# Reordering the join of two spectral transforms, and two moves in the load queue, in an adaLN block on one core

## The chip, the cores and the metric

The kernel runs on one core of a Trainium2 chip. Times are device microseconds of one execution; the median of several is quoted. Two figures occur for one execution: the time (about 253 us) and the span of the profile (about 251 us, from the first to the last instruction). Positions such as "at 84 us" are on the profile's clock.

Engines are named as in the profile: PE is TensorE's matmuls, PEld its weight loads, DVE is VectorE, ACT is ScalarE, POOL is GpSimd, SP the engine that issues most DMAs, SPq its queue.

## The reference, cut to what matters

```python
mod = (_silu(c) @ w_mod).reshape(1, 6, 1, -1)      # sa, ca, ga, sb, cb, gb
h = _layernorm(x) * (1 + ca) + sa
x = x + ga * irfft2(rfft2(h) * (w_r + 1j * w_i))   # "A": spectral filter, 2048 x 640
h = _layernorm(x) * (1 + cb) + sb
x = x + gb * ((silu(h @ w_gate) * (h @ w_up)) @ w_down)   # "B": feed-forward, 640 -> 1728 -> 640
```

The kernel does the forward transform over the rows (to about 36 us), then 21 groups of frequencies pass a *join*: a first-stage product on TensorE, a multiplication by the weights on VectorE, a second stage back (to 63 us). The rest of the inverse transform makes 16 tiles of the new x (to 84 us). Then comes the feed-forward part in five chunks of rows, the first of which is computed in the plain way.

## The kernel before

The queue of loads that SP issues, in order, with cuts. A DMA transpose turns four blocks of the forward transform around. `wm_r` holds modulation weights.

```python
t2_dma(0); t2_dma(1); t2_dma(2)                                   # transposes, used from group 5 on
nc.sync.dma_start(wm_r[:, :, 1:3, :], wm_m[:, :, 1:3, :])         # 1600 KB
t2_dma(3)                                                         # used from group 17 on
nc.sync.dma_start(wm_r[:, :, 3, :], wm_m[:, :, 3, :])
# ... inverse table, w_down (2.2 MB), last gate/up slice ...
load_gu(0, 512)       # columns of w_gate, then of w_up
load_gu(512, 1024)
# ... in the loop over the 16 tiles of x:
if t == 5:
    ln2_tr(0)                # DMA transpose of the first chunk's normalised rows
    load_gu(1024, 1664)
if t in (8, 11):             # GpSimd's queue: sums of weights made by accumulating DMAs
    gu_dma(GS[0][:], B_w_gate, t // 11 * 2, 2, t == 8)
if t in (10, 13):
    ln2_mod(0, range(4) if t == 10 else range(4, 5))   # scaling of the transposed chunk: 4 on GpSimd, 1 on ScalarE
# ... after the loop: four more gu_dma (GS[2] and UG: gate, then up added onto it)
```

The join. `wsum` forms the sum of real and imaginary weights; the half `Wv` comes from a row-flipped copy of the weights that takes a detour through DRAM and lands late.

```python
ga_mod(320, 5, range(3))
t2_pe(0)
wsum(Wv, 48, 64, nc.vector)          # waits for the flipped weights
t2_pe(1)
ga_mod(320, 5, range(3, NC5))        # broadcast of the gate ga, 5 matmuls a half
PPs[0] = stage_a(0)                  # 4 matmuls, then prod(.., 0) with Wn and prod(.., 1) with Wv on VectorE
# ...
PPs[1] = stage_a(1)
ga_mod(0, 6, range(2))
for g in range(NG + 1):
    # ... weight sums for later groups, on GpSimd ...
    if g + 2 < NG:
        PPs[g + 2] = stage_a(g + 2)
    if g == 0:
        ga_mod(0, 6, range(2, NC5))
    # ...
    if g < NG:
        Y2s[g] = stage_b(g, PPs.pop(g))      # 8 matmuls, 1 ScalarE copy
    # ... stage_c, evacuation ...
```

The plain gate/up block of the first chunk takes its 13 slices of 128 columns in the order 0, 6, 1, 7, 2, 8, ...:

```python
for fc in range(NFC - 1):
    ff = fc if fc == 12 else fc // 2 + 6 * (fc % 2)
    half = gu_plain(ci, ATc, ff, (c3f, c22f)[fc % 2])
    half(0)      # 5 matmuls with gate columns
    half(1)      # 5 matmuls with up columns
```

## Time and profile before

| | before |
|---|---|
| time, three runs | 253.23 us median (251.34 to 253.86) |
| span of the profile | 250.8 us |
| TensorE busy, granted clock | 97%, 0.999 |

From the page of the kernel before: busy us of each engine with the share of the span, and the span in 40 slices of 6.3 us (a digit is tenths of busy time; PEclk is the granted clock in tenths).

```profile
PE 243.4 (97%) x2512; PEld 200.1 (80%) x2512; DVE 210.1 (84%) x524; ACT 163.1 (65%) x300; POOL 74.4 (30%) x122
PE   8899998999999999999999999999999999999994
PEclk9999999999999999999999999999999999999999
DMA  7999999999999999500005021002311000211001
```

TensorE is near full throughout, at full clock. The DMA engines are near full until about 100 us (the first 16 digits).

From VectorE's timeline before. Columns: start us, us, engine, line, operation, output<-input, count, and in brackets the idle time before it and what ended it.

```profile
39.27 0.43 DVE L407 TENSOR_TENSOR rW<-rW 128x512 bf16<-128x512 bf16 x1 [1.13 <-DMA rW<-wflip_r]
39.62 5.33 DVE L588 TENSOR_TENSOR rM<-psum,rW 128x384 bf16<-128x384 f32 x12
45.14 4.74 DVE L588 TENSOR_TENSOR rM<-psum,rW 128x384 bf16<-128x384 f32 x10 [0.20 <-PE psum L567]
```

The sum of the late weights (L407) starts when their DMA lands, after 1.13 us of idling; twelve products follow without a break.

From TensorE's timeline before:

```profile
40.68 0.49 PE L567 MATMUL psum<-Ktab,rM 128*128 128x192 bf16 x4 [0.99 <-DVE rM L588]
82.41 0.49 PE L972 MATMUL psum<-rW,Wp 128*128 128x256 bf16 x3
83.22 0.38 PE L972 MATMUL psum<-rW,Wp 128*128 128x256 bf16 x2 [0.32 <-POOL rW L784]
83.98 14.36 PE L984 MATMUL psum<-rW 128*128 128x256 bf16 x130
98.17 7.80 PE L877 MATMUL psum<-rA,rX 128*128 128x320 bf16 x56
```

There is a hole of 0.99 us in the join, and one of 0.32 us inside the last gate/up slice (L972), which waits for GpSimd's scaling. The plain gate/up block (L984) starts at 83.98 and runs its 130 matmuls without a hole: 14.19 us to the first down product.

From the chain of waits before (start us, us, what): the second norm's transpose takes 6.46 us from issue to landing, and GpSimd's scaling follows.

```profile
74.12 6.46 DMA rW<-rL
80.76 0.55 POOL rW L784
81.31 1.87 POOL rW L784 x3
84.15 14.19 PE psum L984 x130
```

From the list of DMA issues before (KB each, us from issue to landing): the fourth transpose, and the last up load (columns 1024 on).

```profile
rM<-rA SPq DMA_TRANSPOSE x1, 10.5
rW<-in_B_w_up_dram SPq DMA_DIRECT2D x1, 800.0 KB, 9.3
```

### The profile page before, as it was taken

How to read it: one execution, taken by the hardware profiler on the slowest of the kernel's cores; microseconds unless marked ns; L12 is line 12 of the kernel's file. 1: busy time of each engine (PE TensorE's matmuls, PEld its weight loads, DVE VectorE, ACT ScalarE, POOL GpSimd, SP SyncE). 2: the span in 40 equal slices, each digit the busy share in tenths (PEclk: the TensorE clock that was granted, in tenths of full speed). 3: DMA queues.
4: the chain of work that ended last, by engine and by line, in shares of the span. 5: the costliest groups of instructions: out<-in, count | busy, mean ns of one | idle time of the engine just before them, and what ended most of it. 6: DMA issues, size and time to landing. Idle time of an engine off the chain costs nothing.

```text
span 250.8 us, 6472 instructions
## 1 busy us (share of the span) xinstructions
PE 243.4 (97%) x2512; PEld 200.1 (80%) x2512; DVE 210.1 (84%) x524; ACT 163.1 (65%) x300; POOL 74.4 (30%) x122
## 2 busy tenths in 40 slices
PE   8899998999999999999999999999999999999994
PEld 3678877999889888788877778886768887779973
DVE  4698888998898997779997997879995888895895
ACT  3678756988788787678963577774257676235740
POOL 8477766677021805000001910001330000440000
PEclk9999999999999999999999999999999999999999
DMA  7999999999999999500005021002311000211001
GB/s 204 400 338 327 308 386 182 269 270 398 301 343 273 238 270 183 119 26 0 3 0 107 0 78 31 3 3 41 77 42 52 3 0 3 52 54 56 3 0 52
DMA packets 45760, 34.43 MB, mean 137 GB/s; under 512 B 21731, under 2 KB 42658, under 8 KB 45346
## 3 DMA queue, kind: packets, MB, share of 16 engines
q1 hardware_dynamic: 43936, 30.00, 42.4%
q0 software_dynamic: 1504, 3.95, 7.0%
q8 instruction: 19, 0.31, 0.5%
q10 hardware_dynamic: 290, 0.08, 0.1%
q14 instruction: 11, 0.09, 0.1%
HBM read 26.72 MB, written 4.72 MB: 125 GB/s over the span
## 4 chain that ended last, share of the span: by engine, by line
PE 68%; DMA 12%; SPq 9%; issue 4%; DVE 2%; POOL 2%; ACT 0%; DVEq 0%; POOLq 0%; ACTq 0%
PE psum L1014 32%; PE psum L897 19%; PE psum L984 9%; DMA rM<-rA 4%; DMA rW<-wflip_r 4%; PE psum L877 3%; DMA rW<-rL 3%; SPq L273 2%; SPq L277 2%; DMA rM<-in_w_mod_dram 2%; SPq L275 2%; PE psum L972 2%; SPq L279 2%; PE psum L595 1%; PE psum L567 1%
## 5 line engine op out<-in xcount | busy, mean ns | idle before, releaser
L1014 PEld LDWEIGHTS <-rW 128*128 128x128 bf16 (+1 forms) x528 | 46.9, 98 | 5.7 <-issue 0.2
L1014 PE MATMUL psum<-rW 128*128 128x256 bf16 (+1 forms) x240 | 27.1, 259 | 0.0
L911 POOL TENSOR_TENSOR rM<-rM,rL 128x320 f32<-128x320 f32 x6 | 5.9, 976 | 68.3 <-ACT rL L910 68.3
L897 PEld LDWEIGHTS <-rE 128*128 128x128 f16 (+1 forms) x196 | 19.1, 97 | 7.7
L1014 PE MATMUL psum<-rY,rW 128*128 128x256 bf16 (+1 forms) x96 | 24.0, 259 | 0.0
L984 PE MATMUL psum<-rW 128*128 128x256 bf16 (+1 forms) x170 | 23.1, 291 | 0.0
L897 PE MATMUL psum<-rE 128*128 128x320 f16 (+1 forms) x147 | 22.3, 299 | 0.0
L588 DVE TENSOR_TENSOR rM<-psum,rW 128x384 bf16<-128x384 f32 (+2 forms) x42 | 20.0, 541 | 1.8 <-PE psum L567 0.9
L984 PEld LDWEIGHTS <-rW 128*128 128x128 bf16 x170 | 16.6, 98 | 3.8
L1014 PEld LDWEIGHTS <-rE 128*128 128x128 f16 x192 | 17.4, 98 | 2.4
L897 PEld LDWEIGHTS <-rX 128*128 128x128 bf16 (+1 forms) x151 | 14.6, 97 | 5.4
L1050 DVE TENSOR_TENSOR rH<-psum,rW 128x512 bf16<-128x512 f32 x21 | 14.5, 690 | 4.9 <-PE psum L1014 3.1
L758 POOL TENSOR_TENSOR rstd<-rstd,mhalf 128x4 f32<-128x4 f32 (+2 forms) x4 | 4.7, 1187 | 46.7 <-DVE rstd L754 46.7
L1046 ACT COPY rH<-psum 128x512 f32<-128x512 f32 x21 | 12.3, 586 | 8.7 <-PE psum L1014 7.0
L1053 ACT COPY rX<-psum 128x512 f32<-128x512 f32 x21 | 12.3, 587 | 6.9 <-PE psum L1014 6.9
L1040 ACT COPY rW<-psum 128x512 f32<-128x512 f32 x21 | 12.3, 586 | 6.8 <-PE psum L1014 6.6
L1068 DVE TENSOR_TENSOR rX<-rH,rL 128x512 bf16<-128x512 bf16 x21 | 8.9, 424 | 9.1 <-ACT rL L1066 9.0
L382 DVE SCALAR_TENSOR_TENSOR rE<-rE,mv,psum 128x648 bf16<-128x648 f32 (+1 forms) x17 | 14.2, 844 | 2.6 <-PE psum L318 1.5
L1054 DVE TENSOR_TENSOR rX<-psum,rX 128x512 f32<-128x512 f32 x21 | 14.4, 685 | 1.7 <-ACT rX L1053 1.6
L897 PE MATMUL psum<-rA,rX 128*128 128x320 bf16 (+1 forms) x98 | 15.6, 299 | 0.0
L1014 PE MATMUL psum<-rH,rW 128*128 128x256 f16 (+1 forms) x96 | 15.1, 259 | 0.1
L1014 PE MATMUL psum<-rE,rY 128*128 128x256 f16 (+1 forms) x96 | 15.1, 259 | 0.0
(198 smaller groups left out, 675.3 us busy)
## 6 DMA issues: line engine op xcount, KB each, us to landing
out_dram<-rA SPq DMA_DIRECT2D x31, 80.0 KB, 1.6
rM<-in_w_mod_dram SPq DMA_DIRECT2D x3, 800.0 KB, 9.8
rX<-in_A_x_dram SPq DMA_DIRECT2D x3, 640.0 KB, 7.9
rA<-in_B_w_down_dram SPq DMA_DIRECT2D x2, 960.0 KB, 9.9
rM<-in_w_mod_dram SPq DMA_DIRECT2D x1, 1600.0 KB, 8.1
rY<-in_B_w_gate_dram POOLq DMA_DIRECT2D x2, 768.0 KB, 7.2
rW<-in_B_w_gate_dram SPq DMA_DIRECT2D x2, 640.0 KB, 8.0
rW<-in_B_w_up_dram SPq DMA_DIRECT2D x2, 640.0 KB, 8.2
```

What stands on the lines that cost most here:

```text
L382: nc.vector.scalar_tensor_tensor(Zv[:, h], Cv[:, h], mv[:, t, 0:1], zps[:, h], ALU.mult, ALU.subtract)
L588: nc.vector.tensor_tensor(PP[:, :, hl], xv[:, :, hl], in1, ALU.mult)
L877: nc.tensor.matmul(pop, lhsT=ATc[rows(k), k, tl * 128:(tl + 1) * 128], rhs=Wd_sb[rows(k), k, 320 * h:320 * h + 320], start=(k == 0), stop= ...
L897: nc.tensor.matmul(o, lhsT=lhsT, rhs=rhs, start=start, stop=stop, skip_group_check=True)
L984: nc.tensor.matmul(gu[u], lhsT=Wgu[:, u, c5, ff * 128:(ff + 1) * 128], rhs=h2T[:, :, c5, :], start=(c5 == 0), stop=(c5 == NC5 - 1))
L1014: nc.tensor.matmul(o[:, f], lhsT=w, rhs=b, start=(start and f == 0 and i == 0), stop=(stop and f == F - 1 and i == len(ops) - 1), skip_gro ...
L1040: nc.scalar.copy(c0, X)
L1046: nc.scalar.copy(c2, X)
L1050: nc.vector.tensor_tensor(c11, Z, c0, ALU.add)
L1053: nc.scalar.copy(c3, X)
L1054: nc.vector.tensor_tensor(c22, Y, c3, ALU.add)
L1068: nc.vector.tensor_tensor(ato, v4(c11), v4(g21), ALU.mult)
```

## The change

The intent is to close those holes: let the first product run before VectorE waits for the late weights, fill TensorE's hole with gate-broadcast matmuls, and bring two transposes forward in the queue by letting two weight loads stand behind them.

```diff
@@ SP's queue
         t2_dma(2)
+        t2_dma(3)
         nc.sync.dma_start(wm_r[:, :, 1:3, :], wm_m[:, :, 1:3, :])
-        t2_dma(3)
@@ stage_a (the modulation columns, which read wm_r[1:3], move to later groups)
-    for c5 in {NG - 6: (0, 1), NG - 5: (0, 1), NG - 4: (2, 3), NG - 3: (2,), NG - 2: (4,), NG - 1: (3, 4)}.get(g, ()):
+    for c5 in {NG - 4: (0, 1), NG - 3: (0, 1), NG - 2: (2, 3, 4), NG - 1: (2, 3, 4)}.get(g, ()):
...
             prod(g, PP, xps, 0)
+            if g == 0:
+                wsum(Wv, 48, 64, nc.vector)
             prod(g, PP, xps, 1)
@@ the join
         t2_pe(0)
-        wsum(Wv, 48, 64, nc.vector)
...
-        ga_mod(0, 6, range(2))
+        ga_mod(0, 6)
         for g in range(NG + 1):
...
+            if g == 0:
+                Y2s[0] = stage_b(0, PPs.pop(0))
             if g + 2 < NG:
                 PPs[g + 2] = stage_a(g + 2)
-            if g == 0:
-                ga_mod(0, 6, range(2, NC5))
...
-            if g < NG:
+            if 0 < g < NG:
                 Y2s[g] = stage_b(g, PPs.pop(g))
@@ gate/up loads
     load_gu(0, 512)
-    load_gu(512, 1024)
...
                 ln2_tr(0)
+                load_gu(512, 1024)
                 load_gu(1024, 1664)
```

(One single-column weight sum on GpSimd also moves from before the loop into its first turn; GpSimd's order of work stays the same.)

More of the change, by code (lines that the diff above doesn't have):

```diff
@@ L682, in adaln_block_kernel @@
         wsum(Wn, 80, 81, nc.gpsimd)
-        wsum(Wv, 80, 81, nc.gpsimd)
         PPs[1] = stage_a(1)
-        ga_mod(0, 6, range(2))
+        ga_mod(0, 6)
         for g in range(NG + 1):
             sa_add(g + 4 if g > 0 else 0)
-            for W, lo, hi in {0: ((Wv, 0, 16),), 1: ((Wv, 16, 32),), 3: ((Wv, 32, 48),), 11: ((Wn, 64, 80),), 13: ((Wv, 64, 80),)}.get(g, ()):
+            for W, lo, hi in {0: ((Wv, 80, 81), (Wv, 0, 16)), 1: ((Wv, 16, 32),), 3: ((Wv, 32, 48),), 11: ((Wn, 64, 80),), 13: ((Wv, 64, 80),)}.get(g, ()):
                 wsum(W, lo, hi, nc.gpsimd)
+            if g == 0:
+                Y2s[0] = stage_b(0, PPs.pop(0))
             if g + 2 < NG:
                 PPs[g + 2] = stage_a(g + 2)
-            if g == 0:
-                ga_mod(0, 6, range(2, NC5))
             if g == NG - 3:
```

## The prediction

> **What bounds it now.** The granted clock is 0.999 throughout and TensorE is busy 97% of a 250.8 us span (page, part 1). From about 84 us on the chain of waits is TensorE nearly alone; the gain must come from TensorE's holes before 84 us. By the timeline of TensorE these are: 0.99 us ahead of the third first-stage group at 40.68 us (released by VectorE's product); 0.25 us ahead of group 17 at 56.29; and 0.48 us lost inside the five matmuls of the last gate/up slice at 82.4 to 83.4.
>
> **What the change moves, costed from the trace.**
> 1. VectorE idles 1.13 us up to 39.27 behind the late weights' sum (released by the flipped weights' DMA), though the first product needs only the other weights, and its matmuls end near 38.5. Engine queues are first in, first out (Trainium skill, "TensorE: Matmul & The Clock Gate", specification table: VectorE strict FIFO); the trace agrees, with nothing run in the 1.13 us. The product (0.49 us) now fits in that hole: the next products start about 0.45 us earlier.
> 2. Three gate-broadcast matmuls (0.41 us) move ahead of the join into TensorE's 0.99 us hole. But the first backward group (8 matmuls, 0.45 us) now precedes the third first-stage group, so VectorE may wait some 0.2 us for it. From 45 to 61 us TensorE is 99%, VectorE and ScalarE 89% busy (table by stretches), so part of this may not be kept. Net: 0.4 to 0.8 us.
> 3. The fourth transpose waits behind a 1.6 MB load: issue to landing 10.5 us, against 4.4 to 6.1 for the others; group 17's correction on GpSimd follows its landing at 55.9. The ring is served in order (Trainium skill, "DMA: Bandwidth & Descriptors", Queues, rings and completion order); this long landing agrees. It should now land near 49 to 50 us. The load swaps places, landing near 54.5 instead of 52.6; its readers (the modulation columns, same count of matmuls) move two groups later, to about 55.2. Net: 0.25 us of TensorE, with 0.7 us of slack, estimated.
> 4. The 1.3 MB gate/up load leaves the queue ahead of the second norm's first transpose (issue to landing 6.46 us, GpSimd's scaling follows at 80.76 to 83.17, TensorE waits for it). The transpose should land in 3.5 to 4.5 us, and the 0.48 us goes. Cost: those weights now come after the transpose, landing near 81 to 83 us; the second gate/up slice needs them at about 84. The last third is wanted near 88 and should land at 86 to 88.
>
> **Sum.** 0.6 (1, 2) + 0.25 (3) + 0.4 (4) = about 1.2 us. 253.2 - 1.2 = 252.0 us; 80% range 250.3 to 253.5. The runs before scatter by 2.5 us, more than the effect. Faster by over 2%: 0.04; within 2%: 0.95; slower by over 2%: 0.01.
>
> **What would show it.** Timeline: a product on VectorE near 38.6, before the sum at 39.27; TensorE's hole at 40 shrunk by about half; the fourth transpose 4 to 6 us to landing, no hole before group 17; no wait of the last slice on GpSimd; the plain gate/up block starting near 82.8 instead of 83.98, without holes.
>
> **What would make it wrong.** The modulation matmuls waiting for the swapped load at 55 us; gate/up slices waiting for late weights at 84 to 88 us; ScalarE pacing the join, so 1 and 2 vanish; or scatter hiding it all.

## The result, and the profile after

The changed kernel is correct and slower: 259.26 us median of six runs (258.01 to 259.97), against 252.83 us (251.34 to 253.86, six runs). The ratio is 1.0258, with a 95% interval of 1.0209 to 1.0306. Here and below a ratio is the mean time of one kernel's runs over that of the other's in the same rounds, so it is not quite the ratio of the medians. Executions over 1.5% slower than the fastest of the same kernel are left out of the means.

From the page after:

```profile
PE 246.4 (96%) x2512; PEld 201.5 (78%) x2512; DVE 210.6 (82%) x524; ACT 163.1 (63%) x300; POOL 74.4 (29%) x122
PE   8999998999999739999999999999999999999994
PEclk9999999999999977999999999999999999999999
DMA  6999989999979999010000411000511000211001
```

There are two new things: a hole in TensorE at the fourteenth and fifteenth digit (about 84 to 97 us), and a fall of the granted clock just after it. The DMA row also shows a thinner digit (7) at about 71 to 77 us.

From TensorE's timeline after:

```profile
81.48 0.71 PE L971 MATMUL psum<-rW,Wp 128*128 128x256 bf16 x5
82.57 6.17 PE L983 MATMUL psum<-rW 128*128 128x256 bf16 x55
94.35 11.27 PE L983 MATMUL psum<-rW 128*128 128x256 bf16 x75 [5.61 <-DMA rW<-in_B_w_up_dram]
105.45 6.85 PE L876 MATMUL psum<-rA,rX 128*128 128x320 bf16 x49
```

The last slice (L971) no longer waits, and the plain block starts 1.41 us earlier than before (82.57 against 83.98). But after 55 matmuls (five slices and the gate half of the sixth, the first slice with columns from 1024 on) TensorE waits 5.61 us for up weights. The other 75 matmuls then take 11.1 us to the first down product; at the pace of before (14.19 us for 130) they would take 8.2 us.

From the list of DMA issues after, and the chain of waits after: the fourth transpose lands in half the time, and the up load, issued at 77.09, lands 17.2 us later instead of 9.3.

```profile
rM<-rA SPq DMA_TRANSPOSE x1, 5.4
rW<-in_B_w_up_dram SPq DMA_DIRECT2D x1, 800.0 KB, 17.2
77.09 17.21 DMA rW<-in_B_w_up_dram
```

The account closes. From the start of the plain block to the first down product it was 14.19 us before and is 22.88 us after (105.45 - 82.57), 8.69 us more; the block starts 1.41 us earlier; the difference is 7.28 us, and the spans differ by 258.0 - 250.8 = 7.2 us.

The table by stretches shows where the DMA time went. Columns: stretch, its length, then busy us (count) of PE, PEld, DVE, ACT and POOL, granted clock, DMA share, GB/s. First before, then after.

```profile
71.00:73.50 2.50, 2.50 (x39) 2.35 (x37) 2.34 (x8) 1.82 (x5) 1.50 (x2) 1.00 1.09 369
84.00:89.00 5.00, 5.00 (x49) 4.48 (x47) 4.80 (x15) 4.17 (x10) 2.75 (x4) 1.00 0.92 168
```

```profile
71.00:73.50 2.50, 2.50 (x37) 2.20 (x35) 2.44 (x7) 2.29 (x5) 1.04 (x2) 1.00 0.30 66
84.00:89.00 5.00, 4.74 (x44) 4.01 (x41) 4.96 (x15) 4.67 (x10) 1.55 (x3) 1.00 1.08 240
94.00:100.00 6.00, 5.65 (x27) 4.03 (x28) 2.08 (x5) 1.48 (x4) 1.98 (x2) 0.50 1.14 186
```

With the gate/up load out of the way, the queue runs nearly dry for 2.5 us ahead of the transpose: 66 GB/s instead of 369, so (369 - 66) x 2.5 us = 0.76 MB of traffic is put off into the stretch where it is wanted. And from 94 to 100 us the clock is granted at one half.

### The profile page after: what moved, and what is told of

It reads as the page before. It is cut to its first block, busy times and chain, and to the rows that moved or that the text cites. A ratio compares the mean times of both kernels' runs of the same rounds, so it can differ in the third digit from the quotient of the medians.

```text
span 258.0 us, 6472 instructions
## 1 busy us (share of the span) xinstructions
PE 246.4 (96%) x2512; PEld 201.5 (78%) x2512; DVE 210.6 (82%) x524; ACT 163.1 (63%) x300; POOL 74.4 (29%) x122
## 4 chain that ended last, share of the span: by engine, by line
PE 68%; DMA 7%; issue 4%; DVE 2%; ACT 1%; SPq 1%; POOL 1%; DVEq 0%; POOLq 0%; ACTq 0%
PE psum L1013 32%; PE psum L896 18%; PE psum L983 7%; DMA rW<-in_B_w_up_dram 7%; PE psum L876 3%; PE psum L597 3%; PE psum L567 2%; PE psum L618 1%; PE psum L971 1%; DVE rM L1151 1%; SPq L732 1%; DVE rE L635 0%; PE psum L571 0%; DVE rM L590 0%; POOL rstd L757 0%
## 5 line engine op out<-in xcount | busy, mean ns | idle before, releaser
L983 PE MATMUL psum<-rW 128*128 128x256 bf16 (+1 forms) x170 | 26.1, 316 | 5.6 <-DMA rW<-in_B_w_up_dram 5.6
L1013 PE MATMUL psum<-rW 128*128 128x256 bf16 (+1 forms) x240 | 27.1, 259 | 0.0
L983 PEld LDWEIGHTS <-rW 128*128 128x128 bf16 x170 | 18.0, 107 | 11.1 <-DMA rW<-in_B_w_up_dram 5.9
L382 DVE SCALAR_TENSOR_TENSOR rE<-rE,mv,psum 128x648 bf16<-128x648 f32 (+1 forms) x17 | 14.2, 844 | 2.1 <-PE psum L318 1.5
```

What stands on the lines that cost most here:

```text
L382: nc.vector.scalar_tensor_tensor(Zv[:, h], Cv[:, h], mv[:, t, 0:1], zps[:, h], ALU.mult, ALU.subtract)
L983: nc.tensor.matmul(gu[u], lhsT=Wgu[:, u, c5, ff * 128:(ff + 1) * 128], rhs=h2T[:, :, c5, :], start=(c5 == 0), stop=(c5 == NC5 - 1))
L1013: nc.tensor.matmul(o[:, f], lhsT=w, rhs=b, start=(start and f == 0 and i == 0), stop=(stop and f == F - 1 and i == len(ops) - 1), skip_gro ...
```

## The experiments

Theory A: the moved gate/up load alone costs the time, through late up weights. Rival B: the reordered join or the moves around the fourth transpose cost it.

### Undo the one move

```diff
 # changed kernel
     load_gu(0, 512)
+    load_gu(512, 1024)
...
                 ln2_tr(0)
-                load_gu(512, 1024)
                 load_gu(1024, 1664)
```

> The changed kernel with one part undone: the gate/up load of columns 512 to 1023 goes back in front of the second norm's first transpose. Theory A (the moved load brings the last third's up weights after they are wanted): the 5.6 us wait of TensorE in the plain gate/up block and the half-speed clock after it both go, and the time falls from 259 to about 252.3 us, a few tenths under the kernel before. Rival B (the reordered join or the other two queue moves cost the time): the time stays near 258 to 259 us.

Measured: 252.71 us against 253.08 before in the same rounds; ratio 0.9976 (0.9923 to 1.0028). The loss is gone. From its TensorE timeline:

```profile
83.43 0.38 PE L972 MATMUL psum<-rW,Wp 128*128 128x256 bf16 x2 [0.43 <-POOL rW L784]
84.20 14.36 PE L984 MATMUL psum<-rW 128*128 128x256 bf16 x130
```

The block runs without a hole, and the wait on GpSimd's scaling is back. Rival B falls.

### The one move alone

```diff
 # kernel before
     load_gu(0, 512)
-    load_gu(512, 1024)
...
                 ln2_tr(0)
+                load_gu(512, 1024)
                 load_gu(1024, 1664)
```

> The kernel before with only the gate/up load of columns 512 to 1023 moved behind the transpose. Theory A: about 259 to 260 us, with a wait of 5 to 7 us of TensorE for the up weights of columns 1024 on, in the sixth slice of the plain block. Rival B: about 252.5 us, no wait.

Measured: 260.48 us against 253.08; ratio 1.0281 (1.0228 to 1.0333). TensorE's timeline has the same hole:

```profile
95.63 9.87 PE L983 MATMUL psum<-rW 128*128 128x256 bf16 x75 [6.06 <-DMA rW<-in_B_w_up_dram]
```

The move is both enough and needed for the loss. Here 75 matmuls after a longer hole took 9.7 us to the first down product (at 105.34), not 11.1. The tables by stretches of both profiles show why. Columns as above; first the changed kernel, then the move alone:

```profile
93.00:94.00 1.00, 0.00 (x0) 0.00 (x0) 0.00 (x0) 0.00 (x0) 0.17 (x1) 0.75 0.14 45
100.00:101.00 1.00, 1.00 (x10) 0.81 (x9) 1.00 (x2) 0.26 (x1) 0.00 (x0) 0.83 1.13 218
```

```profile
91.00:92.00 1.00, 0.00 (x0) 0.00 (x0) 0.00 (x0) 0.10 (x2) 0.00 (x0) 0.97 1.18 419
98.00:99.00 1.00, 1.00 (x7) 0.75 (x6) 0.01 (x1) 1.00 (x3) 0.00 (x0) 0.62 1.05 184
```

All stretches between the two of a pair have 0.50. So the clock was low from about 93.5 to 100.3 us in one and from 91.9 to 98.8 us in the other, 6.8 us in both (worked out from the means of the edge stretches). TensorE worked through 6.0 us of it in the first, but through only 3.1 us in the second, as the hole there ended at 95.63: at half clock that costs about half of it, 3.0 and 1.6 us, near the 2.9 and 1.5 us by which the 75 matmuls were slow.

### Keep TensorE busy in the wait

Theory C: part of the loss is the clock, which falls because TensorE stands idle. Matmuls on constants, into the bank that the waiting product is about to overwrite, fill the hole.

```diff
                 half(0)
+                if fc == 5:
+                    for _ in range(50):
+                        nc.tensor.matmul(half.gu1, lhsT=ones[:], rhs=ones[:].unsqueeze(1).to_broadcast([P, 2, 128]),
+                                         start=True, stop=True)
                 half(1)
```

> The changed kernel with 50 matmuls on constant data (about 5.4 us at full clock), their result overwritten, put on TensorE just before the matmul that waits for the late up weights. Theory C (of the loss, 5.6 us is the wait itself and about 3 us is the clock granted at half speed after it, because TensorE stood idle): the wait shrinks to a few tenths, the granted clock stays at 1.0, and the time falls by about 3 us, to 256 us. Rival (the clock falls for another reason, or the block after the wait is slow because of late data): 259 us or more.

Measured: 258.06 us against 253.08; ratio 1.0201 (1.0140 to 1.0261). The time missed the expected 256 us. The move alone took 260.48 us in the same rounds, 2.4 us more, but that kernel lacks the reordered join. One of the four executions had a mean clock of 0.992 and took 259.78 us; the others, at 0.999 to 1.0, took 257.48 to 258.59 us. The profile, with clock 0.999, is clearer than the time:

```profile
83.50 6.17 PE L983 MATMUL psum<-rW 128*128 128x256 bf16 x55
95.27 8.36 PE L983 MATMUL psum<-rW 128*128 128x256 bf16 x75
103.47 4.80 PE L876 MATMUL psum<-rA,rX 128*128 128x320 bf16 x34
```

The last 75 matmuls take 8.2 us, the pace of full clock, instead of 11.1: the clock's part is 2.9 us. The stretch from block start to down products is 103.47 - 83.50 = 19.97 us, against 22.88. The total gained less than that: everything ahead of the block ran 0.93 us later in this execution (83.50 against 82.57), and the up weights with it (landing near 95.2 instead of 94.3 us); and in later chunks, between 146 and 175 us, TensorE lost another 0.8 us against the changed kernel, for which no cause was looked for. 2.91 - 0.93 - 0.8 is the 1.2 us between the spans (258.0 and 256.8).

The Trainium skill, "TensorE: Matmul & The Clock Gate", "What's actually happening", says that the clock drops to half after one idle window of about 3.4 us. The runs agree in kind: a hole of 5.61 us brought 0.50, a hole of 1.19 us (two experiments below) left the profiled execution at 1.0. But with the move alone TensorE stood still from 89.57 us and the clock fell at 91.9 us, after 2.4 us, sooner than the page's figure; in the changed kernel it fell after some 4.8 us.

### Take the competing loads away

Why does the up load take 17.2 us? GpSimd's loads travel in the same stretch: the second one, which adds, and the first two of the last four, which are plain copies (the last two, which add, are issued at 93.8 us or later). Theory A1: sharing the engines with them slows it. Rival A2: its place in its own queue suffices.

```diff
-            if t in (8, 11):
+            if t == 8:                       # second accumulating load dropped: wrong on purpose
...
-        for o, n, r, w in (...): gu_dma(...)        # after the tile loop
+                if fc == 7:                  # in the plain block; the memset makes the loads wait for VectorE
+                    nc.vector.memset(GS[2][:, :, 0:1], 0.0)
+                    for o, n, r, w in (...): gu_dma(...)
```

> The changed kernel with the accumulating gate/up loads of GpSimd's queue taken out of the stretch in which the late up weights travel: the second of the first pair is dropped (the result is wrong on purpose), the last four wait for the eighth slice of the plain block. Theory A1 (the late landing is mostly sharing: the up load had 0.8 MB in 8.5 us while GpSimd's loads ran): the up load of columns 1024 on lands within 9 to 10 us of its issue instead of 17.2, the wait goes, and the plain block starts and runs without a hole; the time is about 251.5 to 254 us unless the last four loads now come late for the next chunk. Rival A2 (its place behind 2.1 MB in its own queue decides): it lands 14 us or more after issue and a wait of 3 us or more remains.

Measured: 250.17 us, but the run is not what it was meant to be: the moved loop's variable `n` overwrote the chunk's number of tiles, 28 down products were left out and a tile was never written (not a number in the result). Only its landing counts: 10.5 us. The time is void. It was repeated with other variable names:

> The run before this without its slip (a loop variable of the moved loads overwrote the number of tiles, so 28 of the 56 down products of the first chunk were left out and one tile was never written). Otherwise the same: the second accumulating load dropped (wrong on purpose), the last four of GpSimd's loads held until the eighth gate/up slice. Sharing theory A1: up load of columns 1024 on lands 9 to 11 us after issue, plain block without a hole for 14.2 us, 56 down products after it; time 251 to 254 us. Rival A2 (place in its own queue): landing 14 us or more, a hole of 3 us or more.

Measured: 251.64 us against 251.87; ratio 0.9983 (0.9949 to 1.0017); the result is wrong as intended. From its DMA issues and TensorE's timeline:

```profile
rW<-in_B_w_up_dram SPq DMA_DIRECT2D x1, 800.0 KB, 10.2
83.11 14.35 PE L983 MATMUL psum<-rW 128*128 128x256 bf16 x130
```

With the load still behind the transpose and behind 2.1 MB of its own queue, it lands 10.2 us after issue and nothing waits. The late place alone would not have cost anything: it needed the sharing. Rival A2 falls. The reverse, sharing without the late place, was not tried: in the kernel before the up load landed after 9.3 us, but there GpSimd's second load was issued only at 83.12 us.

The Trainium skill, "DMA: Bandwidth & Descriptors", "Queues, rings and completion order", says that each DMA engine goes round robin between the queues it has work for. That agrees in kind: between the landing of the gate load (76.52 + 9.3 = 85.8 us) and its own at 94.3 us, the 800 KB (0.82 MB) up load moved at about 96 GB/s, an estimate from these landings, while the engines moved 263 GB/s in that stretch. This shows that the engines were shared, not in which turns.

### Want the late columns later

```diff
-                ff = fc if fc == 12 else fc // 2 + 6 * (fc % 2)
+                ff = fc
```

> The changed kernel with the plain block's slices taken in rising order, so that columns from 1024 on are first read in the ninth slice instead of the sixth (3.3 us later). If the loss is only the lateness of those weights (landing near 94.3 us on the profile's clock): the hole shrinks from 5.6 to about 2.4 us, and the part at half clock after it with it; time about 254 to 256.5 us. If the hole is something else: 259 us.

Measured: 253.83 us against 251.87; ratio 1.0082 (1.0037 to 1.0128), a little less than expected.

```profile
94.17 5.09 PE L983 MATMUL psum<-rW 128*128 128x256 bf16 x45 [1.19 <-DMA rW<-in_B_w_up_dram]
55.91 0.40 PE L571 MATMUL psum<-sc_col,rM 128*128 128x1 bf16 x10 [0.48 <-DMA rM<-in_w_mod_dram]
```

The hole shrinks to 1.19 us and the clock of the profiled execution stays at 1.0 (another, not profiled, had 0.990 and took 255.68 us). The up load took 16.0 us from issue. The second line is another wait that the prediction had named as a risk: the modulation matmuls wait 0.48 us for the load that changed places with the fourth transpose. The profile of the changed kernel shows no such wait, but it is not alone: of the nine profiles of kernels with the swapped load, those of the undone move (weight load of these matmuls: 0.31 us), of the first run without sharing (0.36 us) and of the last kernel below (0.3 us) have it too.

### Two repairs

The first keeps the load in front and mends the rest: one scaling goes from GpSimd to ScalarE, and stage_a(2) again precedes stage_b(0).

```diff
 # e1_load_back
-            if ci == 0 and c5 < 4:           # on GpSimd
+            if ci == 0 and c5 < 3:
...
-                ln2_mod(0, range(4) if t == 10 else range(4, 5))
+                ln2_mod(0, range(3) if t == 10 else range(3, 5))
...
-            if g == 0:
-                Y2s[0] = stage_b(0, PPs.pop(0))
             if g + 2 < NG:
                 PPs[g + 2] = stage_a(g + 2)
...
-            if 0 < g < NG:
+            if g < NG:
```

> The changed kernel with the gate/up load back in front, and two more edits: the fourth scaling of the first transposed chunk on ScalarE instead of GpSimd, and the third first-stage group again ahead of the first backward group. Theory: the 0.43 us wait of the last gate/up slice on GpSimd falls to under 0.1 us without moving any load; in the join the second batch of products starts 5.5 us after the late weights' sum starts, against 5.75 with the changed order and 5.87 before (so the changed order itself had given 0.2 us back). Time about 252.0 us, 0.4 to 0.9 us under the kernel before. Rival: ScalarE's copies of the last tiles are late by the added 0.6 us, and the wait only changes its name.

Measured: 251.93 us against 251.87; ratio 0.9997 (0.9966 to 1.0028). The expected 0.4 to 0.9 us did not show.

```profile
81.77 0.71 PE L970 MATMUL psum<-rW,Wp 128*128 128x256 bf16 x5
83.25 14.36 PE L982 MATMUL psum<-rW 128*128 128x256 bf16 x130
```

The rival was right about the scaling: the five matmuls of the last slice run without a wait, but from their start to the plain block it is still 1.48 us (1.57 before, 1.09 after the change), because ScalarE's copy for the last tile came later (TensorE's next matmul waits 0.20 us for it). The join's second batch of products started 5.53 us after the sum, as expected.

The second leaves the load behind the transpose, takes rising slices, and holds GpSimd's last four loads back:

```diff
-                ff = fc if fc == 12 else fc // 2 + 6 * (fc % 2)
+                ff = fc
...
+                if fc == 5:
+                    nc.vector.memset(GS[2][:, :, 0:1], 0.0)
+                    for o_, n_, r_, w_ in (...): gu_dma(...)      # moved here from after the tile loop
```

> The changed kernel (gate/up load left behind the transpose) with rising slices and the last four of GpSimd's loads held until the sixth slice; nothing dropped, the result is right. If lateness and sharing are the whole cause, the up load lands near 89 to 90 us, before its first use at about 91.5 us: no hole, clock 1.0, time about 252.2 us. If the second accumulating load alone slows it as much, a hole of 1 to 3 us remains.

Measured: 251.74 us against 251.87; ratio 0.9994 (0.9957 to 1.0031), correct.

```profile
rW<-in_B_w_up_dram SPq DMA_DIRECT2D x1, 800.0 KB, 14.2
83.49 14.36 PE L983 MATMUL psum<-rW 128*128 128x256 bf16 x130
```

There is no hole; the load landed near 92.1 us, later than expected, just in time for the ninth slice. So of the 7 us between 17.2 and 10.2, holding the last four loads back saves 1.8 us (against rising slices, 16.0, the only other difference) to 3.0 us (against 17.2), and dropping the second load (while holding the others a little longer) some 4 us more. These are single profiles. The others fall in with them: the move alone 17.7 us and the filler 17.2 us, the void run 10.5 us, the kernel below 14.0 us.

| kernel | up load, issue to landing | hole of TensorE |
|---|---|---|
| before | 9.3 us | none |
| after | 17.2 us | 5.61 us |
| rising slices | 16.0 us | 1.19 us |
| rising slices, last four held | 14.2 us | none |
| second dropped, last four held (slices in the old order) | 10.2 us | none |

### All that helped, together

The last kernel with stage_a(2) ahead of stage_b(0).

> Everything that helped in a profile put together: the changed kernel with rising slices, the last four of GpSimd's loads held until the sixth slice, and the third first-stage group again ahead of the first backward group. By the profiles: second batch of products 5.5 us after the late weights' sum starts (5.87 before), no wait of the last slice on GpSimd (0.32 us before), no hole in the plain block. Sum about 0.8 to 1.0 us under the kernel before, ratio 0.996 to 0.997. If the scatter of the flipped weights' landing hides it, a ratio of 1.000 with an interval of 0.003 either side.

Measured: 251.85 us against 253.55 (252.82 without the two slow runs); ratio 0.9964 (0.9911 to 1.0018), correct. The plain block starts at 82.67 without a hole. The ratio is the expected one, but the interval holds 1: it is not shown to be faster than the kernel before.

## Why the prediction was wrong, point by point

**Items 1 and 2, the join: the mechanism of 1 was right, the size was not.** ("Engine queues" is said there of VectorE, the engine that the cited row is about.) From VectorE's timeline after, and from TensorE's:

```profile
37.85 0.56 DVE L590 TENSOR_TENSOR rM<-psum,rW 128x384 bf16<-128x384 f32 x1 [0.43 <-PE psum L567]
38.72 0.43 DVE L407 TENSOR_TENSOR rW<-rW 128x512 bf16<-128x512 bf16 x1 [0.30 <-DMA rW<-wflip_r]
39.18 5.11 DVE L590 TENSOR_TENSOR rM<-psum,rW 128x384 bf16<-128x384 f32 x11
44.47 4.74 DVE L590 TENSOR_TENSOR rM<-psum,rW 128x384 bf16<-128x384 f32 x10 [0.18 <-PE psum L567]
```

```profile
39.79 0.64 PE L597 MATMUL psum<-identb,rM 128*128 128x128 bf16 x8 [0.41 <-DVE rM L590]
41.87 0.33 PE L567 MATMUL psum<-Ktab,rM 128*128 128x192 bf16 x2 [0.22 <-DVE rM L590]
42.80 0.41 PE L567 MATMUL psum<-Ktab,rL 128*128 128x192 bf16 x3 [0.16 <-DVE rM L590]
```

One product does run ahead of the sum. The start of the sum differs by 1.2 us between profiles, so all is counted from there. The second batch of products starts 5.87 us after it before (45.14 - 39.27), and 5.75 us after the change (44.47 - 38.72): 0.12 us gained, not 0.4 to 0.8. One product of 0.444 us (5.33 / 12) left the line. But the next one starts 0.46 us after the sum instead of 0.35 (it needs the sum's result, which the product that used to follow did not): 0.11 us back. And eleven products take 5.11 us, where eleven times 0.444 is 4.88: 0.23 us back. The two runs with stage_a(2) in front started the second batch at 5.53 us, so that 0.22 us is indeed the price of the backward group put first; item 2 had named it ("some 0.2 us"). The figures repeat: 5.86 us with the move alone, which has the old join, and 5.74 to 5.77 us in all seven profiles with the new one. The three broadcast matmuls filled TensorE's hole, which shrank from 0.99 to 0.41 us as forecast, but two new holes of 0.22 and 0.16 us follow, all released by VectorE: it set the pace, and nothing was gained that can be seen. From the sum's start to the end of the join (the next gate broadcast) it was 23.85 us before and 23.47 after, so item 3 and the rest of the join brought at most 0.26 us more. Even that is not safe: with the move alone, whose join is the old one, it was 23.59 us.

**Item 3, the fourth transpose: the landing was right, the gain is not shown.** It landed in 5.4 us, near 49.4 us, and the hole ahead of group 17 is gone. But the hole is gone in the profile of the move alone too, where the old order of the queue happened to land the transpose in 8.6 us. And the swapped load, which landed at 54.6 us as forecast, had not 0.7 us of slack but 0.3: its first reader, a weight load, starts at 54.87 us. In four of nine profiles its readers waited 0.3 us or more, which undoes the gain of 0.25 us.

**Item 4, the second transpose: gain right, cost wrong. This is the step that failed.** The transpose landed in about 4.2 us (from 73.19 us to the start of GpSimd's scaling at 77.41), inside the forecast, and the 0.48 us at the last slice went, as predicted: from the end of the join to the plain block it took 20.38 us instead of 20.86, and 20.38 or 20.39 us in all eight profiles with the load behind the transpose. The failing sentence is "The last third is wanted near 88 and should land at 86 to 88." It was wanted near 88.7 and landed at 94.3. Three things were missing from the estimate; it does not say how it was made. It named nothing of GpSimd's loads, though they share the engines; without them the load lands in 10.2 us, at 87.3 us, which would have been inside the stated range. It missed that earlier scaling frees GpSimd's own queue: the second accumulating load was issued at 79.53 instead of 83.12 us, into the very stretch. And it did not see that the emptied queue would leave the engines at 66 GB/s for 2.5 us. How much each of the last two adds by itself was not tried apart.

**The half clock was not in the prediction at all.** A wait was priced as a wait. The profile shows 5.6 us of waiting and 2.9 us of slow matmuls after it.

**The sum.** The predicted gains of 1.2 us came out as 0.38 (join and fourth transpose, in this pair of profiles) + 0.48 (last slice) = 0.86 us; the remaining 0.55 us of the block's earlier start is the earlier sum (38.72 against 39.27), for which no cause was found. That the block started at 82.57 us, near the forecast 82.8, is therefore in part luck. The loss is 5.6 us of hole, 2.9 us of half clock and 0.2 us in which the last matmul before the hole ran out, 8.7 us in all. The prediction named late weights under "what would make it wrong", but gave "slower by over 2%" a chance of 0.01: the named risk had no price.

What stays open: why the flipped weights land at different times in different executions, and whether any of the repaired kernels beats the one before; their gains are within the intervals.

## What to carry to other kernels

A load that is moved back in a saturated queue must be checked against the time at which its last byte is wanted, with everything that other queues issue in that stretch counted, including what the change itself sets free earlier. A wait of some microseconds on TensorE can cost more than its length, since the clock can fall with it (2.9 us on top of 5.6 here, 1.5 on top of 6.1 with the move alone, nothing seen on top of 1.2); if it can't be avoided, want the late data later (an order of slices took most of this loss away) or hold back competing loads that nobody needs yet. And a bottleneck engine relieved of one instruction gives part of it back when the order now puts a dependent instruction, or a longer step of another engine, directly behind.

## What the Trainium skill lacked or had wrong

- "DMA: Bandwidth & Descriptors", "Queues, rings and completion order", gives round robin between queues, but no size for what a plain load loses beside GpSimd's loads: here the same 800 KB load landed about 10, 14 or 16 to 18 us after issue, with none, one or three of the competing loads near it.
- The same page does not say that moving a load out of a full queue can leave the engines nearly idle ahead of a transpose that is not ready yet: 66 GB/s instead of 369 for 2.5 us.
- "TensorE: Matmul & The Clock Gate", "What's actually happening", gives one idle window of about 3.4 us before the clock falls; here it fell 2.4 us after TensorE stopped in one profile and 4.8 us in another. The runs add the price beside one hole: the low clock lasted 6.8 us in both, and cost 1.5 or 2.9 us by how much of it TensorE had work for.
